# Gate logits of two chunks on VectorE instead of TensorE, and a new order in the later part

## The chip, the cores and the metric

The kernel runs on one core of one Trainium2 chip. The metric is the device time of the whole program in microseconds, as the median of several executions. The core has a matrix engine (TensorE, PE in the profile), a vector engine (VectorE, DVE), a scalar engine (ScalarE, ACT), GpSimd (POOL) and SyncE (SP). Each takes its instructions in order from a queue of its own. Here SP issues nearly all of the transfers, and PEld is the loading of TensorE's stationary operand.

## The reference, cut to what matters

```python
def A(x, wqkv, wo):                     # S = 2048 rows, D = 1024, 32 heads of 32
    q, k, v = heads(x @ wqkv)
    # row s looks at rows s, s-2, ..., s-14 (8 of them); rows before 0 are masked
    attn = softmax(einsum("bhsd,bhswd->bhsw", q, gather(k)) * 32 ** -0.5)
    return einsum("bhsw,bhswd->bhsd", attn, gather(v)).reshape(B, S, D) @ wo

def B(x, w_gate, w_up, w_down):         # Df = 3584
    return (gelu(x @ w_gate) * (x @ w_up)) @ w_down

g = sigmoid((x * gate_w).sum(-1, keepdims=True))   # one number for each row
return g * A(x) + (1 - g) * B(x)
```

All arrays are bfloat16. The change is about `(x * gate_w).sum(-1)`, the gate's logit, and about the order of the work around it.

## The kernel before, in words

The 2048 rows are cut into four chunks of 512 rows, and each chunk into four blocks of 128 (`NST`). Chunks are worked on in pairs, called sup 0 (chunks 0 and 1) and sup 1 (chunks 2 and 3). The large products use a scheme with seven products of half-size blocks in place of eight. It needs sums of blocks of weights and of x beforehand (the "forms", made on VectorE) and sums of products behind (on VectorE and ScalarE, out of PSUM's eight banks).

`main` (L1618) is TensorE's order: q, k and v of the first pair (`qkv_pair`, matmuls at L836), then the hidden layer of the first pair (`ffn`, 28 tiles f, matmuls at L1214), then the output projection of chunk 0 (`down`, L1496), q, k and v of chunks 2 and 3, the hidden layer's first tiles for sup 1 and the projection of chunk 1, the rest of the hidden layer of sup 1, the projection of chunk 2, and that of chunk 3, which is the last stage.

For each tile f of the hidden layer, VectorE and ScalarE do a short chain. L1246 copies a bank to seed the next, L1298 copies one to `u`, L1302 adds a bank to it, L1306 and L1290 are the GELUs, L1263 multiplies GELU and up part, L1272 copies `m`, and L1281 adds a bank and `m` into `hT`, which also frees that bank for TensorE's product two groups later. L504 makes the weights' forms in the ring slots (for sup 0 from raw weights that come with L403; GpSimd stores the forms with L513, and sup 1 loads them back).

Attention works on VectorE in the same time: L1015 and L1021 are the products and sums of the scores, L1107 to L1138 the softmax's sums, L1162, L1172, L1176 and L1180 the weighting of v and its sums. Transposes by DMA on SP's queue (L1084, L1153) carry its weights and results from one layout to another. L369 loads x transposed.

The weights go through a ring of 20 slots of 256 KB (`ring_load`, `ring_give`). A slot is given back in a fixed order by the instruction that read it last, and the next load in `loads` (L438) waits on SP's queue until it has one. Each product m of the projection takes nine such loads (seven of w_down or of its forms, two of wo) and 18 matmuls for each of two column groups g. In the last stage, the third product (m = 2) is replaced by seven smaller ones (`inner`, L1385, 256 columns), whose weights come with three loads of their own (L1335, `load_inner`). It is emitted from hooks inside the other products: `head` after the eighth step of m = 3, g = 1, `body` and `join` before m = 4, g = 0, and `end` inside it.

The gate: `gate(c)` (L930) multiplies x transposed with `gate_w` as 16 matmuls of a 32-column operand for two chunks (L938). VectorE (L953) turns the result round, L961 copies the wanted columns to `zq`, `gate_sum` (L966) adds four partial sums by fp32 matmuls for a pair of chunks (L974), and L979 clips them. The exponential of the logit goes with the first softmax of a chunk (`ez`), and L985 to L991 make `omg`, the factor of the output. `gate(2)` and `gate(3)` stand in the projection of chunk 0, ahead of its product m = 5.

The order of all engines is written out by the class `Weave`. Its `run` (L129) holds some streams of operations and picks again and again the operation with the smallest modelled start plus the stream's bias. An operation with a due date loses its bias from `AHEAD` before that date on. So a bias moves a whole stream behind or ahead of others in an engine's queue, and once the program is built, the queues are fixed:

```python
                b = s[0] if op.due is None or t + self.AHEAD < op.due else 0.0
                b = b if op.bias is None else op.bias
                if best is None or t + b < best[0]:
                    best = (t + b, t, s, op)
```

Of the kernel before, what the change touches and what calls it, by code (L numbers as in the profile page):

```python
# [14 lines left out]
P = 128  # L15
# [28 lines left out]
class Weave:  # L44
# [7 lines left out]
    AHEAD = 15.67  # L52
# [76 lines left out]
    def run(self, streams):  # L129
        live = []  # L130
        for bias, g in streams:
            h = next(g, None)
            if h is not None:
                live.append([bias, g, h])
        while live:
            best = None
            for s in live:
# [4 lines left out]
                b = s[0] if op.due is None or t + self.AHEAD < op.due else 0.0  # L142
# [12 lines left out]
def kernel(  # L155
# [71 lines left out]
    DUE = (80.05, 296.5)  # L227
# [180 lines left out]
    def steps_of(c):  # L408
        return (0, 1, 3, 2, 4, 5, 6) if c >= INNER else range(7)

    def load_down(c, first=()):
        for m in range(7):
# [21 lines left out]
    def loads():  # L434
# [15 lines left out]
        for b in range(2, NBLK):  # L450
            yield from load_block(0, b)
            if 4 + 2 * (b - 1) < NPREP:
                yield load_prep(4 + 2 * (b - 1))
        for sup in range(NSUP):
            c0 = 2 * sup
            more = sup + 1 < NSUP
            if more:
# [7 lines left out]
                for b in range(NE // FB, NBLK):  # L465
                    yield from load_block(sup + 1, b)
            else:
# [49 lines left out]
    def x_forms():  # L517
        t = tt(KH * SC)
        for sup in range(NSUP):
# [11 lines left out]
            yield dve(t, lambda b12=b12, b22=b22: V(out=b12, in0=b22, in1=b12, op=ALU.subtract), [("z", cb)], key=("xf", sup, 3), bias=-1.0 if sup else -0.3)  # L531
            yield dve(t, lambda b21=b21: V(out=tf[:, 2], in0=b21, in1=tf[:, 1], op=ALU.subtract), [t2], key=("xf", sup), bias=-1.0 if sup else -0.3)

    gates, logits = {}, {}
# [205 lines left out]
    def qkv_forms():  # L740
        for sup in range(NSUP):
            c = 2 * sup
            t = tt(D)
            for which in QVK if sup else (0, 1, 2):
# [13 lines left out]
                for f in range(4):  # L758
                    for kt in range(0, KH, 2):
# [17 lines left out]
                        if f == 2 and not sup and which == 0:  # L777
# [3 lines left out]
                                 bias=(0.24, -0.6)[which == 0] if which < 2 and not sup else None,  # L781
                                 due=DUE[1] + 17.6 * QVK.index(which) + 3.94 * f if sup else 0.0)
# [147 lines left out]
    def gate(c):  # L930
# [26 lines left out]
        if c % 2 == 0:  # L957
            logits[c // 2] = (small.tile([P, 2, SC // 32], F32, tag="zq", bufs=1, name="zq"),
                              small.tile([P, 2, NST], F32, tag="zc", bufs=1, name="zc"))
        zq, zc = [z[:, c % 2, :] for z in logits[c // 2]]  # L960
        e = dve(0.1, lambda: nc.vector.tensor_copy(out=zq, in_=zt.rearrange("p (b j) -> p b j", j=32)[:, :, 0]), [e],  # L961
                key=("zq", c))
        yield e
        ez = small.tile([P, NST], F32, tag="ez", bufs=2, name="ez")
        omg = small.tile([P, NST], F32, tag="omg", bufs=3, name="omg")
        gates[c] = (ez, omg, zq, zc)  # L966

    def gate_sum(c):
        i, free = bank_take()
        zq, zc = logits[c // 2]  # L970

        def go():
            for q in range(4):
                nc.tensor.matmul(banks[i][32 * q:32 * (q + 1), 0:2 * NST], lhsT=qsum[:],  # L974
                                 rhs=zq[:].rearrange("p c (j q) -> p (c j) q", q=4)[:, :, q], start=True, stop=True,
                                 tile_position=(0, 32 * q), skip_group_check=True)
        o = pe(1, go, [("zq", c), ("zq", c + 1)] + ([free] if free else []))
# [695 lines left out]
```

## Time and profile before

| what | value |
|---|---|
| times of three runs | 716.2, 716.57, 717.89 us (median 716.57) |
| the profiled execution | 718.17 us, of which the span is 716.4 |
| TensorE busy | 707.4 us, 99% of the span, clock 1.0 throughout |
| VectorE busy | 620.9 us, 87%, 908 instructions |
| ScalarE busy | 327.9 us, 46% |
| GpSimd busy | 73.8 us, 10% |
| DMA | 176.84 MB, mean 247 GB/s; SP's queue 69.0% of 16 engines' span |
| gates of chunks 2 and 3 on TensorE | 16 matmuls from 291.85 to 292.83 us |

All times in the profile are microseconds from the start of the span. A group or a timeline row names the line of the kernel, the engine, the operation, what it writes and reads with its shape, and how often; busy times on one engine may overlap by some tens of nanoseconds, since the next instruction starts before the last has left. The chain is followed from the last instruction back to what released each step.

### The profile page before, as it was taken

The numbers are of one execution on the slowest core, as the hardware profiler recorded it, in microseconds if no ns is written. First come the engines' busy times: TensorE is split into PE (matmuls) and PEld (weight loads), VectorE is DVE, ScalarE is ACT, GpSimd is POOL, SyncE is SP. The second block draws the span as 40 slices with busy tenths as digits, with TensorE's granted clock in tenths as the row PEclk, the third lists the DMA queues.
The fourth block names the chain that finished last, engine by engine and source line by source line (L and its number), as shares of the span: only waits on it lengthen the run. The fifth ranks groups of instructions, "written<-read, shape, count | busy, mean of one in ns | idle before, by whom it ended". The sixth has DMA issues, their size and how long they took to land.

```text
span 716.4 us, 9983 instructions
## 1 busy us (share of the span) xinstructions
PE 707.4 (99%) x3317; PEld 348.4 (49%) x3382; DVE 620.9 (87%) x908; ACT 327.9 (46%) x559; POOL 73.8 (10%) x130
## 2 busy tenths in 40 slices
PE   9999999999999999999999999999999999999998
PEld 5566544444444444456664444444444444444464
DVE  4999999899998989899789988799999997868710
ACT  5454685455675522154465323358556655210110
POOL 0040133433112000100000000100000000001000
PEclk9999999999999999999999999999999999999999
DMA  9963789995998699954369799995647756999972
GB/s 269 374 239 100 223 247 332 355 341 209 220 220 252 201 239 339 331 197 146 85 190 301 256 299 356 311 321 171 178 146 188 180 161 162 307 309 370 398 247 101
DMA packets 181971, 176.84 MB, mean 247 GB/s; under 512 B 56224, under 2 KB 138784, under 8 KB 181664
## 3 DMA queue, kind: packets, MB, share of 16 engines
q1 hardware_dynamic: 172304, 145.53, 69.0%
q0 software_dynamic: 9328, 30.42, 11.4%
q8 instruction: 26, 0.43, 0.2%
q10 hardware_dynamic: 288, 0.26, 0.1%
q14 instruction: 25, 0.20, 0.1%
HBM read 132.65 MB, written 31.46 MB: 229 GB/s over the span
## 4 chain that ended last, share of the span: by engine, by line
PE 87%; DMA 5%; issue 3%; DVE 2%; ACT 1%; POOL 0%; SPq 0%; DVEq 0%; POOLq 0%; ACTq 0%
PE ps L1214 40%; PE ps L1496 27%; PE ps L836 18%; DMA lend<-in_A_x_dram 2%; DMA ring<-in_B_w_gate_dram 1%; PE ps L605 1%; DMA ring<-in_B_w_down_dram 1%; DMA hT<-in_A_wqkv_dram 1%; DMA hT<-in_A_wo_dram 1%; DMA fforms<-ring 0%; DVE ring L504 0%; PE ps L1385 0%; DVE xbuf L1172 0%; POOL fforms L513 0%; ACT hT L1256 0%
## 5 line engine op out<-in xcount | busy, mean ns | idle before, releaser
L1214 PEld LDWEIGHTS <-ring 128*128 128x128 bf16 x1568 | 153.2, 98 | 186.7 <-issue 2.8
L1214 PE MATMUL ps<-lend,ring 128*128 128x512 bf16 x878 | 210.9, 379 | 1.4 <-ACT m L1272 0.4
L1214 PE MATMUL ps<-tf,ring 128*128 128x512 bf16 x658 | 162.7, 379 | 1.1 <-DVE hT L1281 0.3
L1496 PE MATMUL ps<-ring,hT 128*128 128x512 bf16 (+1 forms) x710 | 159.9, 375 | 0.6
L1496 PEld LDWEIGHTS <-hT 128*128 128x128 bf16 x722 | 70.5, 98 | 82.2 <-DVE xbuf L1021 0.4
L836 PEld LDWEIGHTS <-ring 128*128 128x128 bf16 x512 | 65.0, 127 | 46.1 <-issue 1.3
L1162 DVE TENSOR_TENSOR xbuf<-xbuf,lend 128x2048 bf16<-128x2048 bf16 x64 | 77.5, 1216 | 11.4 <-DMA xbuf<-xbuf 11.3
L1015 DVE TENSOR_TENSOR xbuf<-qo,lend 128x2048 bf16<-128x2048 bf16 x64 | 77.0, 1217 | 0.0
L1021 DVE TENSOR_TENSOR xbuf<-xbuf 128x2048 bf16<-128x2048 bf16 x56 | 68.1, 1217 | 0.3
L836 PE MATMUL ps<-tf,ring 128*128 128x512 bf16 x251 | 57.8, 379 | 0.7 <-DVE tf L525 0.5
L836 PE MATMUL ps<-lend,ring 128*128 128x512 bf16 x250 | 57.4, 379 | 0.3
L1246 ACT COPY ps<-ps 128x512 f32<-128x512 f32 x56 | 32.1, 573 | 50.4 <-PE ps L1214 50.3
L1537 ACT ACTIVATE ost<-ps,omg 128x512 bf16<-128x512 f32 x15 | 10.3, 687 | 88.4 <-PE ps L1496 88.4
L1306 ACT ACTIVATE gl<-u 128x512 bf16<-128x512 f32 x56 | 35.4, 632 | 32.0 <-DVE u L1302 31.9
L1496 PE MATMUL ps<-ring,qo 128*128 128x512 bf16 (+1 forms) x191 | 48.9, 375 | 0.3
L1529 POOL DMA_DIRECT2D out_dram<-ost x24 | 13.0, 541 | 341.6 <-ACT ost L1537 252.3
L1290 ACT ACTIVATE gl<-ps 128x512 bf16<-128x512 f32 x56 | 33.5, 599 | 31.7 <-PE ps L1214 31.2
L1263 DVE TENSOR_TENSOR hT<-hT,gl 128x1024 bf16<-128x1024 bf16 x56 | 38.2, 682 | 8.2 <-ACT hT L1256 8.1
L513 POOL DMA_DIRECT2D fforms<-ring x56 | 30.6, 546 | 126.6 <-DVE ring L504 121.4
L504 DVE TENSOR_TENSOR ring<-ring 128x1024 bf16<-128x1024 bf16 x56 | 38.1, 681 | 4.5 <-DMA ring<-in_B_w_up_dram 4.4
L1302 DVE TENSOR_TENSOR u<-ps,u 128x512 f32<-128x512 f32 x56 | 38.3, 683 | 2.8 <-PE ps L1214 2.4
L1172 DVE TENSOR_TENSOR xbuf<-xbuf 128x2048 bf16<-128x2048 bf16 x32 | 38.9, 1215 | 0.1
(149 smaller groups left out, 688.3 us busy)
## 6 DMA issues: line engine op xcount, KB each, us to landing
ring<-dforms SPq DMA_DIRECT2D x105, 256.0 KB, 5.1
ring<-in_B_w_down_dram SPq DMA_DIRECT2D x84, 256.0 KB, 5.3
ring<-in_B_w_gate_dram SPq DMA_DIRECT2D x56, 256.0 KB, 4.5
fforms<-ring POOLq DMA_DIRECT2D x56, 256.0 KB, 5.1
ring<-fforms SPq DMA_DIRECT2D x56, 256.0 KB, 4.0
ring<-in_B_w_up_dram SPq DMA_DIRECT2D x42, 256.0 KB, 4.8
ring<-in_A_wqkv_dram SPq DMA_DIRECT2D x32, 256.0 KB, 3.9
ring<-oforms SPq DMA_DIRECT2D x30, 256.0 KB, 5.5
```

What stands on the lines that cost most here:

```text
L504: nc.vector.tensor_tensor(out=g, in0=ring[:, held[("w", 0, b, x_)], :], in1=ring[:, held[("w", 0, b, y_)], :], op=op)
L836: nc.tensor.matmul(banks[bk][:], lhsT=lhsT, rhs=rhs[:, kt, :], start=(start and kt == 0), stop=(kt == KH - 1), skip_group_check=True)
L1015: V(out=w3(box[t]), in0=q_b, in1=k_w, op=ALU.mult)
L1021: V(out=w3(box[0]), in0=w3(box[0]), in1=w3(box[t]), op=ALU.add)
L1162: return dve(tt(n), taking(("p", t), lambda: V(out=w3(box["p", t]), in0=w3(box["ab"]), in1=v_w, op=ALU.mult)), [("qkv", c, 2, t), abo] + ( ...
L1172: V(out=p0.rearrange("p (u n) -> p u n", u=2), in0=lo, in1=hi, op=ALU.add)
L1214: nc.tensor.matmul(banks[bk][:], lhsT=wv[:, k, fl * P:(fl + 1) * P], rhs=rhs[:, k, :], start=(start and k == 0), stop=(k == KH - 1), skip_ ...
L1263: yield dve(tt(2 * SC), lambda hv=hv, gv=gv: nc.vector.tensor_tensor(out=hv, in0=hv, in1=gv, op=ALU.mult), [e, ev[f, "g1"], ev[f, "g2"]], ...
L1290: nc.scalar.activation(out=gl[f][:, r1 * SC:(r1 + 1) * SC], in_=banks[A[f]][:], func=ACT.Gelu_apprx_tanh)
L1302: e = dve(tt(SC, True), lambda f=f: nc.vector.tensor_tensor(out=u2[f][:], in0=banks[Dk[f]][:], in1=u2[f][:], op=ALU.add), [o, ev[f, "u2"]])
L1306: ev[f, "g2"] = act(0.54, lambda f=f: nc.scalar.activation(out=gl[f][:, r2 * SC:(r2 + 1) * SC], in_=u2[f][:], func=ACT.Gelu_apprx_tanh), [ ...
L1496: nc.tensor.matmul(banks[bk][:, o0:o0 + cols[1] - cols[0]], lhsT=l, rhs=wv[:, i, cols[0]:cols[1]], start=(start and k == 0), stop=(q == la ...
```

## The change: what it does

The logits of chunks 2 and 3 are no longer made from x transposed on TensorE. The rows of x as they lie in memory, four blocks of 128 rows, and `gate_w` repeated for each partition, are loaded into five ring slots for each of the two chunks (`load_rows_of`). VectorE multiplies and sums each block in one call, `tensor_tensor_reduce`, which the built queue shows as two instructions, one over 1024 elements and one over a single element that reads the sum out (`gate_rows`), and clips the four sums. `gate(2)`, `gate(3)` and the second pair's `gate_sum` go; the first pair's `gate_sum` is done for each chunk by itself.

In the last stage, the products are taken in the order 0, 1, 3, 4, 2, 5, 6 rather than 0, 1, 3, 2, 4, 5, 6: the inner product's parts come one product later, its loads stand on SP's queue behind those of m = 3, and the output step L1582 for g = 0 follows the inner join (`joined`).

Last, the streams of `Weave` may have a second bias, which holds from the modelled time 205 us (`TURN`) on; `AHEAD`, a due date and some biases change. By the built queues, VectorE's first 300 or so instructions (to about 205 us) stay nearly as they were and the rest are reordered; GpSimd's queue is the same; on SP's, the transposes L369 of chunks 2 and 3 and the transposes L1084 and L1153 stand a few to ten places later.

```diff
-    AHEAD = 15.67
+    TURN = 205.0
+    AHEAD = 14.59
...
-        for bias, g in streams:
+        for bias, g, *late in streams:
             h = next(g, None)
             if h is not None:
-                live.append([bias, g, h])
+                live.append([bias, g, h, late[0] if late else bias])
...
-                b = s[0] if op.due is None or t + self.AHEAD < op.due else 0.0
+                b = (s[0] if t < self.TURN else s[3]) if op.due is None or t + self.AHEAD < op.due else 0.0
...
-    DUE = (80.05, 296.5)
+    DUE = (80.05, 314.14)
...
     def steps_of(c):
-        return (0, 1, 3, 2, 4, 5, 6) if c >= INNER else range(7)
+        return (0, 1, 3, 4, 2, 5, 6) if c >= INNER else range(7)
 
     def load_down(c, first=()):
-        for m in range(7):
+        for m in (0, 1, 3, 2, 4, 5, 6) if c >= INNER else range(7):
...
         for b in range(2, NBLK):
+            if b == 12:
+                yield from load_rows_of(2)
             yield from load_block(0, b)
...
                 for b in range(NE // FB, NBLK):
                     yield from load_block(sup + 1, b)
+                    if b == 6:
+                        yield from load_rows_of(3)
...
-            yield dve(t, lambda b12=b12, b22=b22: V(out=b12, in0=b22, in1=b12, op=ALU.subtract), [("z", cb)], key=("xf", sup, 3), bias=-1.0 if sup else -0.3)
+            yield dve(t, lambda b12=b12, b22=b22: V(out=b12, in0=b22, in1=b12, op=ALU.subtract), [("z", cb)] if sup == 0 else [], key=("xf", sup, 3), bias=-1.0 if sup else -0.3)
...
-                                 bias=(0.24, -0.6)[which == 0] if which < 2 and not sup else None,
-                                 due=DUE[1] + 17.6 * QVK.index(which) + 3.94 * f if sup else 0.0)
+                                 bias=(0.19, -0.6)[which == 0] if which < 2 and not sup else None,
+                                 due=DUE[1] + 23.67 * QVK.index(which) + 4.11 * f if sup else 0.0)
...
+    def load_rows_of(c):
+        yield ring_load(("gw", c), lambda g: nc.sync.dma_start(out=g, in_=AP(gate_w.tensor, gate_w.offset, [[0, P], [1, D]])))
+        for j in range(NST):
+            yield ring_load(("gx", c, j), lambda g, j=j: nc.sync.dma_start(out=g, in_=x[c * SC + j * P:c * SC + (j + 1) * P, :]))
+
+    def gate_rows():
+        for c in range(2, NCH):
+            zc = small.tile([P, NST], F32, tag="zc", bufs=2, name="zc")
+            ez = small.tile([P, NST], F32, tag="ez", bufs=2, name="ez")
+            omg = small.tile([P, NST], F32, tag="omg", bufs=3, name="omg")
+            gates[c] = (ez, omg, None, zc)
+            for j in range(NST):
+                def dot(c=c, j=j, zc=zc):
+                    r = ring[:, held["gx", c, j], :]
+                    nc.vector.tensor_tensor_reduce(out=r, in0=r, in1=ring[:, held["gw", c], :], scale=1.0, scalar=0.0,
+                                                   op0=ALU.mult, op1=ALU.add, accum_out=zc[:, j:j + 1])
+                o = dve(1.25, dot, [("gx", c, j), ("gw", c)] + ([("ez", c - 2)]), lag=0.5)
+                yield o
+                ring_give(("gx", c, j), o)
+            ring_give(("gw", c), o)
+            yield dve(0.1, lambda zc=zc: nc.vector.tensor_scalar(out=zc[:], in0=zc[:], scalar1=ZMAX, scalar2=-ZMAX, op0=ALU.min,
+                                                                op1=ALU.max), [o], key=("zc", c))
...
-            hk3, hk4 = {7: (head,)}, {0: (body, join), 5: (end,)}
+            hk3, hk4 = {7: (head,)}, {0: (body, join, lambda: joined(0)), 5: (end,)}
+
+        def joined(g):
+            j2, om2, box = 2 * g + 1, omg[:, 2 * g + 1:2 * g + 2], []
+            ev[g, "x"] = dve(0.67, lambda: nc.vector.scalar_tensor_tensor(
+                out=ost_tile(box), in0=banks[Bk[g]][:], scalar=om2, in1=m5[g][:], op0=ALU.mult, op1=ALU.add),
+                [ev[g, "m4"], ev[g, "m5"]])
+            yield from evac(ev[g, "x"], j2, 1, box)
...
-            if (m, g) == (5, 0) and c == 0:
-                yield from gate(2)
-                yield from gate(3)
...
-                    o = yield from prod(Bk[g], m, g, False, [ev[g, "seed"]], hooks=hk3 if g else {})
+                    o = yield from prod(Bk[g], m, g, False, [ev[g, "seed"]])
...
+                    ev[g, "m4"] = yield from prod(Bk[g], m, g, False, [ev[g, "u2"]], hooks=hk4 if g else hk3)
+                    if g or c < INNER:
+                        yield from joined(g)
...
         yield from gate_sum(0)
+        yield from gate_sum(1)
...
-        yield from gate_sum(2)
...
-    w.run([(0.0, main()), (0.0, loads()), (0.0, late_x()), (0.0, moves(3)), (0.6, wforms()), (0.0, down_forms()), (0.0, inner_forms()), (0, x_forms()), (1.89, qkv_forms()),
-           (0.12, preps()), (0.03, attention()), (0.23, scores())])
+    w.run([(0.0, main()), (0.0, loads()), (0.0, late_x()), (0.0, gate_rows(), 0.0), (0.0, moves(3)), (0.6, wforms(), 0.04), (0.0, down_forms(), 0.65), (0.0, inner_forms(), -0.06), (0, x_forms(), -0.44), (1.89, qkv_forms(), -0.92),
+           (0.12, preps()), (0.03, attention(), 0.25), (0.23, scores(), 0.58)])
```

## The prediction, made before any run of the changed kernel

> **What bounds the kernel now.** I read the page's busy table first, then the chain by engine, then windows around each place the change touches, then TensorE's and VectorE's timelines there (start, length, line, operation and count, and in brackets the idle time before it and what ended it). Line numbers are those of the kernel before, for the new order too.
>
> ```profile
> PE 707.4 (99%) x3317; PEld 348.4 (49%) x3382; DVE 620.9 (87%) x908; ACT 327.9 (46%) x559; POOL 73.8 (10%) x130
> PE 87%; DMA 5%; issue 3%; DVE 2%; ACT 1%; POOL 0%; SPq 0%; DVEq 0%; POOLq 0%; ACTq 0%
> ```
>
> TensorE is busy 99% of 716.4 us and holds 87% of the chain: a matmul removed is time removed, unless a wait takes its place. Windows (start:end, length, then busy us and counts of PE, PEld, DVE, ACT, POOL, then granted clock, DMA share, GB/s) show how little room VectorE and the DMA have:
>
> ```profile
> 172.00:204.00 32.00, 31.89 (x146) 14.42 (x148) 31.69 (x51) 21.26 (x37) 6.53 (x12) 1.00 0.85 227
> 204.00:228.00 24.00, 23.42 (x106) 10.45 (x107) 21.36 (x29) 13.37 (x24) 4.32 (x8) 1.00 0.90 225
> 228.00:250.00 22.00, 21.89 (x102) 9.99 (x102) 21.97 (x31) 12.50 (x23) 2.16 (x4) 1.00 0.61 199
> 493.00:546.00 53.00, 52.79 (x243) 24.05 (x246) 50.97 (x66) 32.53 (x57) 0.00 (x0) 1.00 0.62 165
> 644.00:682.00 38.00, 37.84 (x176) 17.32 (x178) 29.29 (x41) 4.58 (x7) 2.70 (x5) 1.00 1.05 383
> ```
>
> The new vector work falls at about 205 to 215 us (rows of chunk 2) and about 493 to 503 us (chunk 3). In both VectorE is nearly full. TensorE's own rows at the removed gates and, below them, where it stands near 220 us:
>
> ```profile
> 291.85 1.05 PE L938 MATMUL ps<-lend,gcol 128*32 128x512 bf16 x16
> 292.83 1.47 PE L1496 MATMUL ps<-ring,hT 128*128 128x512 bf16 x6
> ...
> 218.33 1.89 PE L1214 MATMUL ps<-lend,ring 128*128 128x512 bf16 x8
> 220.48 1.89 PE L1214 MATMUL ps<-tf,ring 128*128 128x512 bf16 x8 [0.26 <-DVE hT L1281]
> 222.21 1.89 PE L1214 MATMUL ps<-lend,ring 128*128 128x512 bf16 x8
> 223.93 1.03 PE L1214 MATMUL ps<-tf,ring 128*128 128x512 bf16 x4
> 225.04 1.89 PE L1214 MATMUL ps<-lend,ring 128*128 128x512 bf16 x7
> 227.01 1.89 PE L1214 MATMUL ps<-tf,ring 128*128 128x512 bf16 x8
> ```
>
> In dense stretches one 512-column matmul takes 0.216 us (49 rows of L1496, one record missing, in 10.74 us). So 218.33 + 8 x 0.216 = 220.06 and the next starts at 220.48: 0.42 lost; likewise 0.25 at 224.79 and 0.24 at 226.77, together 0.91 us. VectorE's timeline names the cause: its L504 waited for block 12's weights, and L1263 and L1281 stood behind it.
>
> ```profile
> 213.52 0.68 DVE L1302 TENSOR_TENSOR u<-ps,u 128x512 f32<-128x512 f32 x1
> 216.80 0.69 DVE L504 TENSOR_TENSOR ring<-ring 128x1024 bf16<-128x1024 bf16 x1 [2.60 <-DMA ring<-in_B_w_up_dram]
> 219.75 0.68 DVE L1281 TENSOR_TENSOR hT<-ps,m 128x512 bf16<-128x512 f32 x1
> ```
>
> **The change, part by part.**
>
> *Gate products gone.* The 16 matmuls hold TensorE from 291.85 to 292.83: **-0.98 us**, on the path. The second gate_sum, at 381 us, goes; the one at 57 us becomes two of four matmuls each, every matmul half as wide (8 took 0.18 to 0.25 us): 0, bounds -0.2 to +0.2. Entering another tile shape may give back a bubble under 0.1.
>
> *Vector work.* Gone: two StreamTransposes (708 ns) and two copies (174 ns), 1.8 us with their gaps. New: eight dots and two clips, one clip more at the start. A dot is two instructions in the built queue, a 1024-element pass and a one-element read-out. Its price p is in no row of before. Low end: L504's 1024 bf16 elements start 0.60 apart, and a clip (156 ns) takes about 0.08 of the queue: p = 0.7. High end: two full passes at one element's pace. That pace is 1.04 ns an element, from L1107's 256 f32 elements (416 ns) and L1302's 512 (683): 1.21 us for 1024, starting 1.14 apart; two passes 2.3. I take one pass at that pace plus a read-out, **p = 1.23** (to 1.4 if the read-out waits for the pass to drain), nearest to L1302, which also carries f32 inside. Eight dots, 10 us, less 1.8, make about 8 us more in VectorE's queue, off the path if the queue has room.
>
> [...] The trace has L504 starting 0.60 apart with 0.68 busy, so I keep 1.23.
>
> *Has the queue room?* In the new order, from 204.70 (unchanged): L504, L1263, L1281, L504, L504 (5 x 0.60) to 207.70; dot, L1302, dot, dot, L1263, L1281 ends at 209.58 + 3p; TensorE needs that bank at 214.0 (212.29 + 8 x 0.216). Then dot, L1302, clip, L504, L1015 (1.14), L1263, L1162 (1.14), L1281 ends at 214.34 + 4p, needed at 220.06. So p may be 1.4 at both. At 1.23 the ends are 213.3 and 219.3: no new wait, and the 2.60 us hole is filled with dots while L504 of block 12 goes to about 223, behind the L1281 it delayed. Hence the three waits vanish: **-0.9 us** (bounds: 0, if others replace them; -0.91). Late next is L504 of block 12 itself.
>
> *Transfers of the rows.* Ten loads of 256 KB join SP's queue, five ahead of block 12 in sup 0, five behind block 6 in sup 1; each holds a ring slot until its dot is done. Block 12's last weights were issued at 211.29 and took 7.22 us (the chain's row):
>
> ```profile
> 211.29 7.22 DMA ring<-in_B_w_gate_dram
> ```
>
> They landed at 218.5. The rows find a place on SP's queue where L369's four transposes (195.47 to 201.05) and nothing else stood, but their slots come back only as the dots end, from 208.9 to 213.9, and SP's issues at 207.58 and 211.89 (3.00 and 3.53 us for two loads) show that it waits for slots. I put block 12's last issue 0.7 to 2.6 us later, landing 219.2 to 221.1, against a need at about 223. If all 1.31 MB lay ahead of it at the stretch's 225 GB/s, it would land at 224.3. Cost 0 (bounds 0 and 1.3 us of VectorE with L1263 and L1281 behind it, all of which TensorE may feel).
>
> Near 500 us the order is L1302, L1138, dot, L1263, L1281, dot, dot, L1302, dot, clip, L1263, L1281. From L1302 at 494.93 the two L1281 end at 498.4 and 503.9 (p = 1.23); TensorE needs them at 500.33 and 506.38: slack 2.0 and 2.4. The rows themselves are issued from 490.2 on and need 4 to 5 us, so the first dot may stand up to 1 us: 0, bounds 0 to +1.
>
> The transposes L369, L1084 and L1153 come up to ten places later on SP; chunk 2's x is needed only at 310 us, and behind L1153 waits L1162, which the order has put later too: 0.
>
> *Last stage.* Before 682 us TensorE has no gap (37.84 of 38.00), so moving the inner product later frees nothing. The order costs: T4's nine loads are wanted 6.8 us sooner (the head and body, 681.72 to 688.48, now follow), from about 681.7 on, the ninth 3.5 us later; they landed at 678 to 683.7 with the inner loads (3 MB, 7.9 us a piece) ahead of T2, which now go behind it. The same bytes lie ahead of T4, in another order: slack 1.5 to 3 us, cost 0, bounds -0.1 to +3. The scores' half of attention gets a bias that ends it about 4.5 us later, at 662.7 for a need at 666.18: covered. L1582's two "x" operations move behind the inner join; L1588's copy still follows the second.
>
> *New order and due dates.* Up to 205 us VectorE's queue is the same but for a few places, so the waits there (0.56 at 138.8, 0.22 at 197) stay. After 228 us its instructions are reshuffled; TensorE's rows there are dense before, so order can gain at most the 0.09 us at 552.8 and the small waits of L836 and L1496, under 1 us. The 8 us more of vector work push attention later there, each L1281 having about 2 us of slack: 0 (bounds -0.9 to +3, a stage's slack lost twice).
>
> **Sum.** -0.98 - 0.9 + 0.1 (bubble) = -1.8 us. The profiled execution took 718.17 us (span 716.4 and 1.8 around it): 716.4 after. It lies 1.6 above the median 716.57, so by the median: **714.8 us**.
>
> **Rivals.**
> *A. Gates only:* the waits at 220 us are replaced by ones like them (L504 late behind the rows). For it: DMA share 0.90 there, SP waiting for slots. Time 716.57 - 1.0 = 715.6.
> *B. Dots too dear (the slower side):* past p = 1.41, L1281 near 219 ends late, 0.4 us for each 0.1 on p; past 1.83 the second one near 504, at the same rate. Against the forecast's -1.8 stands 4 x (p - 1.41) + 4 x (p - 1.83): it decides from p = 1.85, passes +0.3% at 2.1, and gives 716.57 - 1.8 + 3.6 + 1.9 = 720.2 at the high end of 2.3. For it: the operation is in no row, and multiplies and adds. Against: L1302's slope.
> *C. Transfers late:* block 12's weights behind the rows, or T4's in the last stage, by 1 to 5 us beyond their slack: 715.8 to 719.8. For it: share 1.05 in 644 to 682, T2's loads landing as little as 0.7 us ahead of use. Against: the same bytes lie ahead of T4 as before.
> *D. More than forecast:* the new order also takes the small waits after 228 us: 713.0 to 714.4.
> *E. The new order leaves one operation late after 228 us,* where VectorE has 21.97 of 22.00 us busy: up to +3, so 715.6 to 717.8, or 719 if it happens in both pairs of chunks. Against: each of its operations there keeps 2 us.
> *F. The gates were hidden anyway:* excluded, 291.85 to 292.83 is on the chain.
>
> **How the numbers follow.** Forecast 0.40 (own range 713.8 to 715.4), A 0.18, B 0.10, C 0.14, D 0.10, E 0.08. About 0.3% (2.15 us; below 714.42 or above 718.72) is what a measurement of this kernel can tell from no change. Faster: half of the forecast (0.21) and D: 0.31. Slower: most of B (0.07), of C (0.10) and half of E (0.05): 0.22. The rest, 0.47, is within. The low end 713.8 cuts off most of D, 719.2 the ends of B and C; together under 2 in 10.
>
> **What would show it.** No L938 at 292 us, the next product there 1 us sooner; a dot's pair of rows with 1.21 us and a short one, at 1.2 to 1.3 apart; no hole on VectorE at 214 and no wait of L1214 for L1281 at 220; TensorE busy about 706.4. Wrong if the dot takes 1.6 or more, if VectorE stands for ring loads near 222 or 500, or if L1496 waits for a ring load near 681.

## The result, and the profile after

Over 22 executions of each kernel on the same chip the changed kernel took 715.0 us against 716.96 us before (medians). The ratio is 0.9974, with a 95% interval of 0.9964 to 0.9984. That is 0.26% faster: inside the 0.3% that the prediction called no change, and 0.2 us from the time it gave. That it came out so close is partly luck: two of the terms were wrong in opposite directions. The profiled execution took 714.28 us. From here on, lines of the changed kernel have its own numbers: L1238 is the L1214 of before, L1305 is L1281, L1326 is L1302, L1287 is L1263, L509 is L504, L1520 is L1496, L1186 is L1162, and L985 is the new dot.

The page after, busy table and chain by engine:

```profile
span 712.5 us, 9977 instructions
PE 704.5 (99%) x3300; PEld 347.7 (49%) x3366; DVE 631.5 (89%) x920; ACT 329.7 (46%) x559; POOL 74.1 (10%) x130
PE 95%; DMA 3%; issue 1%; SPq 0%; ACT 0%; DVE 0%
```

TensorE carries the chain even more (95%, where it was 87%). VectorE is busy 10.6 us longer (631.5 us, where it was 620.9) and the time still went down. VectorE's timeline where chunk 2's rows are worked on:

```profile
205.12 1.22 DVE L985 CUSTOM_DVE_ANT_0 ring<-ring 128x1024 bf16<-128x1024 bf16 x1
206.27 0.08 DVE L985 DVE_READ_ACCUMULATOR2_ANT zc<- 128x1 f32 x1
206.27 0.68 DVE L1326 TENSOR_TENSOR u<-ps,u 128x512 f32<-128x512 f32 x1
...
209.76 0.68 DVE L1305 TENSOR_TENSOR hT<-ps,m 128x512 bf16<-128x512 f32 x1
...
211.95 0.69 DVE L1326 TENSOR_TENSOR u<-ps,u 128x512 f32<-128x512 f32 x1 [0.38 <-PE ps L1238]
...
216.18 0.69 DVE L1305 TENSOR_TENSOR hT<-ps,m 128x512 bf16<-128x512 f32 x1
```

The dot's pass takes 1.22 us, and the read-out and the next instruction both start 1.15 us after its start: p, the price of a dot in VectorE's queue, is 1.15, and the read-out costs the queue nothing. There is no hole behind L1326. L1305 ends at 210.44 and 216.87. TensorE's timeline in the same place, and where the gates were:

```profile
216.87 1.89 PE L1238 MATMUL ps<-lend,ring 128*128 128x512 bf16 x8
218.59 1.89 PE L1238 MATMUL ps<-tf,ring 128*128 128x512 bf16 x8
220.32 1.89 PE L1238 MATMUL ps<-lend,ring 128*128 128x512 bf16 x8
...
289.38 3.18 PE L1520 MATMUL ps<-ring,hT 128*128 128x512 bf16 x14
292.41 1.03 PE L1520 MATMUL ps<-ring,qo 128*128 128x512 bf16 x4
293.27 2.97 PE L1520 MATMUL ps<-ring,hT 128*128 128x512 bf16 x13
```

Eight matmuls are 1.73 us here, so nothing is lost at 218.59 and 220.32. From 58 us to the last stage this execution has no stop of TensorE of 0.03 us or more. The spans differ by 3.9 us, twice what the medians differ by, so about 2 us of that are not the change. Walking both timelines shows which: TensorE was already 0.65 us ahead at 57 us, and stops of 0.11, 0.56, 0.09 and 0.13 us between 132 and 200 us, in a part of the queues that the change leaves nearly alone, are in the profiled execution of before and not in that of after. Such stops come with the execution and not with the kernel: of eleven profiled executions whose queues are nearly the same up to 200 us, three (this one and two of the experiments) have those at 139, 197 and 200 us, 0.6 to 0.8 us together, and eight have none of them.

### The profile page after: what moved, and what is told of

Read it like the earlier page. It is cut to its first block, busy times and chain, and to the rows that moved or that the text cites. A ratio compares the mean times of both kernels' runs of the same rounds, so it can differ in the third digit from the quotient of the medians.

```text
span 712.5 us, 9977 instructions
## 1 busy us (share of the span) xinstructions
PE 704.5 (99%) x3300; PEld 347.7 (49%) x3366; DVE 631.5 (89%) x920; ACT 329.7 (46%) x559; POOL 74.1 (10%) x130
## 4 chain that ended last, share of the span: by engine, by line
PE 95%; DMA 3%; issue 1%; SPq 0%; ACT 0%; DVE 0%
PE ps L1238 47%; PE ps L1520 28%; PE ps L841 18%; DMA ring<-in_A_wqkv_dram 1%; DMA lend<-in_A_x_dram 1%; PE ps L1409 1%; DMA hT<-in_A_x_dram 1%; DMA ring<-dforms 0%; PE ps L610 0%; SPq L439 0%; DVE tf L530 0%; PE ps L943 0%; ACT ost L1634 0%; ACT it L1425 0%; PE ps L1000 0%
## 5 line engine op out<-in xcount | busy, mean ns | idle before, releaser
L1238 PEld LDWEIGHTS <-ring 128*128 128x128 bf16 x1568 | 153.4, 98 | 184.9
L1238 PE MATMUL ps<-lend,ring 128*128 128x512 bf16 x878 | 210.9, 379 | 0.9
L1238 PE MATMUL ps<-tf,ring 128*128 128x512 bf16 x659 | 162.9, 379 | 0.7
L1520 PE MATMUL ps<-ring,hT 128*128 128x512 bf16 (+1 forms) x706 | 160.0, 375 | 0.8
L1520 PEld LDWEIGHTS <-hT 128*128 128x128 bf16 x722 | 70.6, 98 | 82.0
L1186 DVE TENSOR_TENSOR xbuf<-xbuf,lend 128x2048 bf16<-128x2048 bf16 x64 | 77.7, 1217 | 2.7 <-DMA xbuf<-xbuf 2.5
L1520 PE MATMUL ps<-ring,qo 128*128 128x512 bf16 (+1 forms) x192 | 49.1, 375 | 0.2
L1287 DVE TENSOR_TENSOR hT<-hT,gl 128x1024 bf16<-128x1024 bf16 x56 | 38.2, 683 | 5.6 <-ACT hT L1280 5.4
L1326 DVE TENSOR_TENSOR u<-ps,u 128x512 f32<-128x512 f32 x56 | 38.4, 686 | 3.5 <-PE ps L1238 2.5
L1305 DVE TENSOR_TENSOR hT<-ps,m 128x512 bf16<-128x512 f32 x56 | 38.3, 684 | 2.4 <-PE ps L1238 2.2
L1322 ACT COPY u<-ps 128x512 f32<-128x512 f32 x56 | 32.8, 586 | 15.5 <-PE ps L1238 15.5
L1196 DVE TENSOR_TENSOR xbuf<-xbuf 128x2048 bf16<-128x2048 bf16 x32 | 38.9, 1216 | 0.1
```

Of the source, the lines that this page charges most:

```text
L1186: return dve(tt(n), taking(("p", t), lambda: V(out=w3(box["p", t]), in0=w3(box["ab"]), in1=v_w, op=ALU.mult)), [("qkv", c, 2, t), abo] + ( ...
L1196: V(out=p0.rearrange("p (u n) -> p u n", u=2), in0=lo, in1=hi, op=ALU.add)
L1238: nc.tensor.matmul(banks[bk][:], lhsT=wv[:, k, fl * P:(fl + 1) * P], rhs=rhs[:, k, :], start=(start and k == 0), stop=(k == KH - 1), skip_ ...
L1287: yield dve(tt(2 * SC), lambda hv=hv, gv=gv: nc.vector.tensor_tensor(out=hv, in0=hv, in1=gv, op=ALU.mult), [e, ev[f, "g1"], ev[f, "g2"]], ...
L1305: ev[f, "up2"] = dve(tt(SC, True), lambda f=f: nc.vector.tensor_tensor(out=hs(f, 1), in0=v3(banks[Bk[f]][:]), in1=v3(m5[f][:]), op=ALU.add ...
L1322: nc.scalar.copy(out=u2[f][:], in_=banks[Bk[f]][:])
```

## Experiments

The theory taken into them is the prediction's: each part does its own share, that is, the gates' products and the waits at 220 us go with the gate part, and the order and the last stage's move are worth nothing. The rivals: the waits go because of the order; they were in the one profiled execution only; or the last stage's move pays.

**The gate part alone**

```diff
# before, with gate(2), gate(3) and gate_sum(2) out; load_rows_of, gate_rows and gate_sum(1) in
-    w.run([(0.0, main()), (0.0, loads()), (0.0, late_x()), (0.0, moves(3)), ...
+    w.run([(0.0, main()), (0.0, loads()), (0.0, late_x()), (0.0, gate_rows()), (0.0, moves(3)), ...
```

> The kernel before with the gate part alone: logits of chunks 2 and 3 from rows on VectorE, gate_sum for each chunk by itself, the old biases and the old last stage. Parts theory (each part does its own share): TensorE loses 1.07 us of products and bubbles at 292 us and 0.27 us at 381 us, and pays 0.06 at 57 us; and the dots fill VectorE's hole at 214 us, so the 0.9 us of waits at 219 to 227 us are gone: 2.2 us under the kernel before, and TensorE's timeline dense from 219 to 228 us. Order theory (the waits go because of the new biases): only 1.3 us under before, with waits of L1214's products near 220 us left. Chance theory (the waits at 220 us came up in the one profiled execution only): 1.3 us under before, with no wait near 220 us.

Measured: 715.59 us against 717.11, ratio 0.9984 (0.9974 to 0.9994): 1.15 us under by the ratio and 1.5 by the medians, not 2.2. No wait is left near 220 us, but there are four new ones, 0.24 us at 242 (for L504's form), 0.12 and 0.17 at 556 and 562, and 0.29 in the last stage near 675 us. The chain in the last stage of this kernel:

```profile
670.72 5.29 DMA ring<-oforms
...
676.05 1.24 PE ps L1519 x5
```

The load of wo's forms for m = 3 landed late. SP had stood from 657.89 to 661.22 with the inner product's load (L1335 of before) at its head, whose buffer attention used until 661.20; in the kernel before attention was done with it at 656.99. By the clock the forms are not later than in the kernel before (issued at 670.05 after 671.19), but TensorE comes to the head of the inner product 2.2 us sooner, and SP gained only half of that. So the gate part takes TensorE's products away and pays for some of it in waits that the kernel before has not.

**The last stage's move alone**

```diff
-        return (0, 1, 3, 2, 4, 5, 6) if c >= INNER else range(7)
+        return (0, 1, 3, 4, 2, 5, 6) if c >= INNER else range(7)
...
-        for m in range(7):
+        for m in (0, 1, 3, 2, 4, 5, 6) if c >= INNER else range(7):
# and the hooks of head, body, join and end, and joined(g), as in the change
```

> The kernel before with the last stage's third product behind its fifth, and nothing else. Parts theory: 0, within 0.3 us, since TensorE's rows are dense before 690 us in both kernels; the loads for the fifth product land in time. Rival (the move is what pays): 0.5 us or more under before. Rival (the order of the loads costs, and the other parts hide it): 0.5 us or more over, with waits of L1496's products for ring loads near 682 us. Up to 640 us this is the queue of before, so its profile is also a second look at the waits at 132 to 200 us and at 219 to 227 us: the parts theory expects the latter 0.9 us again, the chance theory not.

Measured: 716.67 us against 717.11, ratio 0.9993 (0.9982 to 1.0004): no difference that these runs can tell. Its profile is worth more than its time, since up to 640 us it is the queue of before, seen once more. Its timelines of VectorE and TensorE:

```profile
214.81 0.69 DVE L504 TENSOR_TENSOR ring<-ring 128x1024 bf16<-128x1024 bf16 x1 [1.88 <-DMA ring<-in_B_w_up_dram]
...
217.75 0.68 DVE L1281 TENSOR_TENSOR hT<-ps,m 128x512 bf16<-128x512 f32 x1
```

```profile
217.14 1.89 PE L1214 MATMUL ps<-lend,ring 128*128 128x512 bf16 x8
218.87 1.89 PE L1214 MATMUL ps<-tf,ring 128*128 128x512 bf16 x8
...
289.86 1.05 PE L938 MATMUL ps<-lend,gcol 128*32 128x512 bf16 x16
290.84 2.33 PE L1496 MATMUL ps<-ring,hT 128*128 128x512 bf16 x10
```

VectorE has the same hole, 1.88 us in place of 2.60, but the stop of TensorE behind it is gone. Of the 0.91 us that the prediction removed near 220 us, only 0.11 us (at 224.7) is there, and of the 0.89 us between 132 and 200 us nothing. The chance theory is right for most of it.

**The changed kernel with the old last stage**

```diff
-        return (0, 1, 3, 4, 2, 5, 6) if c >= INNER else range(7)
+        return (0, 1, 3, 2, 4, 5, 6) if c >= INNER else range(7)
# load_down's order, the hooks and the output step back as before
```

> The changed kernel with the old last stage. Parts theory: as the changed kernel, 2.0 us under before, within 0.3 us. If the last stage's move pays only together with the new order (attention ends later there), this is 0.5 us or more over the changed kernel, with a wait near 666 or 682 us.

Measured: 716.04 us against 717.11, ratio 0.9983 (0.9972 to 0.9994), where the changed kernel has 0.9974; the two intervals overlap, so the profile has to say whether it is real. SP's timeline, VectorE's end of attention, and the chain:

```profile
658.06 1.12 SPq L431 DMA_DIRECT2D ring<-in_A_wo_dram  x2
662.42 1.52 SPq L1359 DMA_DIRECT2D xbuf<-dforms  x2
```

```profile
661.18 1.22 DVE L1196 TENSOR_TENSOR xbuf<-xbuf 128x2048 bf16<-128x2048 bf16 x1
```

```profile
672.13 5.36 DMA ring<-oforms
...
677.54 1.24 PE ps L1520 x5
```

SP was done with the loads ahead at 659.18 and stood until 662.42: the inner product's load (L1359) needs a buffer of attention's, and attention's L1196 ended at 662.40. Behind it on the same queue stand the nine loads for m = 3, which then come late: three stops of 0.19, 0.25 and 0.25 us at 676 to 677.5 us. That this is real rests on the row at 662.42 and on the same hold in the run of the gate part alone, more than on the time. The profiled execution took 717.38 us, 1.3 above its median, and TensorE stops for 1.6 us more ahead of 640 us, 0.97 of it here:

```profile
456.19 2.36 DVE L1186 TENSOR_TENSOR xbuf<-xbuf,lend 128x2048 bf16<-128x2048 bf16 x2 [4.40 <-DMA xbuf<-xbuf]
```

```profile
467.07 1.89 PE L1238 MATMUL ps<-lend,ring 128*128 128x512 bf16 x8 [0.81 <-ACT m L1296]
```

Up to there the queues of all engines are those of the changed kernel, whose profile has none of it (there VectorE waited 1.32 us for that transfer, and TensorE not at all): it is this execution. In the kernel before, the same load was issued at 660.06, 0.3 us behind the one ahead of it. The changed kernel has the m = 3 loads in front:

```profile
662.84 1.00 SPq L431 DMA_DIRECT2D ring<-oforms  x2
664.19 1.00 SPq L1359 DMA_DIRECT2D xbuf<-dforms  x2
```

**The inner loads behind m = 3, the products left where they were**

```diff
# on top of the run before
             if m == 2 and c >= INNER:
-                yield from load_inner()
                 continue
...
+            if m == 3 and c >= INNER:
+                yield from load_inner()
```

> The changed kernel with the old last stage, except that the inner product's three loads stand on SP's queue behind the nine loads of m = 3, as in the changed kernel. Queue theory (with attention later, the inner loads wait for their buffer at the head of SP's queue and hold up the loads of m = 3 behind them; moving the loads is what the last stage's move is worth): no wait of L1496's products near 676 us, and the time of the changed kernel, about 0.7 us under the run with the old last stage. Rival (the product itself has to come later, because its forms are then late): the wait goes from 676 us to the head at about 681 us, and the time is that of the run with the old last stage or more.

Measured: 714.83 us against 716.88, ratio 0.9974 (0.9963 to 0.9985), as the changed kernel. No stop from 58 us to the last stage. The profile bears the queue theory out: what the last stage's move is worth is three loads put behind nine others, and no gain is seen from the product coming later. By the times alone the two runs can't be told apart (0.9983 and 0.9974, overlapping intervals).

**The changed kernel without its order part**

```diff
-    TURN = 205.0
-    AHEAD = 14.59
+    AHEAD = 15.67
...
# DUE, the due dates, 0.19 and all second biases back as before
```

> The gate part and the last stage's move with the old biases, AHEAD and due dates: the changed kernel without its order part. By the run of the gate part alone, which had waits of 0.24 us at 241 us (for a form, L504), 0.12 and 0.17 at 556 and 562 us and 0.29 at 675 us, the last of these should go and the others stay: 0.4 to 0.6 us over the changed kernel, 1.4 to 1.6 under before. If the order part is worth nothing here: as the changed kernel. If it is worth more than these waits show: 1 us or more over it.

Measured: 715.31 us against 716.88, ratio 0.9978 (0.9970 to 0.9987), 0.3 us over the changed kernel by the ratio and by the medians, a little less than expected and within the noise. Its profile has no stop near 675 us, the 0.24 us at 241 us again, and 0.47, 0.10, 0.13 and 0.09 at 465 to 556 us. Up to the last stage VectorE's, ScalarE's and SP's queues are those of the gate part alone, so the two profiles show one order twice: the 0.24 at 241 and 0.09 to 0.12 near 556 us are in both, 0.3 us together. The others are in one of them only, and the stop near 465 us, again for ScalarE's copy `m`, stood in the changed kernel with the old last stage too, whose order is the new one.

**The order part alone**

```diff
# before, with TURN, AHEAD = 14.59, the due dates and
-    ... (0.6, wforms()), (0.0, down_forms()), ... (0.03, attention()), (0.23, scores())])
+    ... (0.6, wforms(), 0.04), (0.0, down_forms(), 0.65), ... (0.03, attention(), 0.25), (0.23, scores(), 0.58)])
```

> The kernel before with the second biases, TURN, AHEAD and the due dates alone. Its queue still has two L504 ahead of the L1281 that was late at 220 us. Parts theory: the waits near 220 us stay in some form, 0.3 to 0.9 us of them, and the time is that of before within 0.5 us. Order theory: the waits are gone, 0.9 us under before. A third way: the biases were set for a queue with the dots in it, and without them something else is late: up to 2 us over before, with a wait on TensorE that the kernel before has not.

Measured: 749.38 us against 717.11, ratio 1.0449 (1.0429 to 1.0469). The third way, and more than ten times its size. What TensorE waited for, in that kernel's waits by line (total, times, longest; L1455 is the forms of the projection, L1454 of before):

```profile
PE ps L1497 <- DVE qo L1455: 14.4, 3, 6.6
PE ps L1497 <- DVE hT L1455: 7.8, 1, 7.8
```

**The same with the late bias of the projection's forms at 0**

```diff
-    ... (0.0, down_forms(), 0.65), ...
+    ... (0.0, down_forms()), ...
```

> The order part alone, as in the run that took 749 us, but without the late bias of 0.65 for the projection's forms (down_forms, L1454 of the kernel before), which goes back to 0 throughout. Starving theory: that run's waits of the projection's products for these forms (1.9 us at 298, 7.9 at 429, 6.7 at 461 and 6.2 at 654 us) come because attention, at a late bias of 0.25, is taken first as long as some of it is ready; without the 0.65 they go, and the time is 716 to 721 us. Rival (attention itself is late by the other biases, and the forms wait for it): the waits stay in the main, 735 us or more.

Measured: 741.73 us against 717.19, ratio 1.0333 (1.0298 to 1.0367). Both theories hold half. None of the four waits for the forms is left, so these were starved by the late bias; but attention now ends late instead, and the last stage waits for it (L1181 writes attention's result):

```profile
PE ps L1497 <- DVE qo L1181: 13.0, 2, 9.7
PE ps L1497 <- DMA ring<-dforms: 5.2, 1, 5.2
```

The biases give a good order only to the set of operations they were written beside. Why attention falls behind without the dots was not followed further.

**A dearer dot, twice**

```diff
+                    for _ in range(1):      # range(2) in the second run
+                        V(out=r, in0=r, in1=r, op=ALU.min)
                     nc.vector.tensor_tensor_reduce(out=r, in0=r, ...
```

> The changed kernel with one more VectorE instruction ahead of each dot, the minimum of a row block with itself (1024 bf16 elements, 0.60 us of the queue each by L504's pace), which leaves the data as it is: a dot then takes 1.15 + 0.60 = 1.75 us of the queue. The prediction's sum put the threshold at 1.41 and so expects 4 x 0.34 = 1.4 us near 219 us. The trace after has the dots' chain 1.1 us earlier than that sum, and slack 1.72 at L1281 behind the fourth dot, with 0.5 us of idle time ahead of it: 4 x 0.60 - 0.5 - 1.72 = 0.2 us near 219 us, nothing near 502 us (slack 2.6 against 2.4). Cheap theory (VectorE has room, the dots' price does not matter): 0. If instead the pushed-back attention is what costs: 1 us or more, in places behind 250 us.

> The same with two such instructions ahead of each dot, 2.35 us for each. By the prediction's sum 3.8 us near 219 us and 2.1 near 502 us, 5.9 in all. By the trace after: 4 x 1.20 - 0.5 - 1.72 = 2.6 us near 219 us and 4.8 - 2.6 = 2.2 near 502 us, 4.8 in all, as waits of L1214's products for L1281. Cheap theory: 0 to 0.5. If pushed-back attention costs as well: 6 us or more, with waits behind 250 us or in the last stage.

Measured: one more instruction 717.5 us against 716.88, ratio 1.0013 (0.9998 to 1.0028); two more 725.06, ratio 1.0114 (1.0097 to 1.0131). VectorE's and TensorE's timelines of the first, then TensorE's of the second:

```profile
205.81 0.68 DVE L986 TENSOR_TENSOR ring<-ring 128x1024 bf16<-128x1024 bf16 x1
206.53 1.23 DVE L987 CUSTOM_DVE_ANT_0 ring<-ring 128x1024 bf16<-128x1024 bf16 x1
```

```profile
217.67 1.89 PE L1240 MATMUL ps<-lend,ring 128*128 128x512 bf16 x8
219.97 1.89 PE L1240 MATMUL ps<-tf,ring 128*128 128x512 bf16 x8 [0.41 <-DVE hT L1307]
```

```profile
218.01 2.62 PE L1240 MATMUL ps<-tf,ring 128*128 128x512 bf16 x8 [2.89 <-DVE hT L1307]
220.42 2.89 PE L1240 MATMUL ps<-lend,ring 128*128 128x512 bf16 x8
223.15 1.03 PE L1240 MATMUL ps<-tf,ring 128*128 128x512 bf16 x4
```

The added instruction costs 0.72 us of the queue and not 0.60: the dot, which needs its result, starts 0.72 us behind it (206.53 - 205.81), where instructions that do not need each other's results start 0.60 apart (in the same profile L1328 at 207.68 and the next L986 at 208.28). So p = 1.87 and 2.59. At p = 1.87 the wait near 219 us sits where the sums put it, at L1281's bank (L1307 here): 0.57 us, for 4 x 0.72 - 0.5 - 1.72 = 0.7 by the slack of the trace after. The 0.39 us near 502 us are at another place than the sums had:

```profile
502.68 1.89 PE L1240 MATMUL ps<-lend,ring 128*128 128x512 bf16 x8 [0.23 <-ACT m L1298]
```

TensorE waits there for ScalarE's copy `m` (L1272 of before), which follows the GELU of the `u` that VectorE's L1302 finishes, and three dots stand ahead of that L1302. In the trace after the copy ends at 499.11 and TensorE wants it at 500.91, so 3 x 0.72 - 1.80 = 0.36 us. That L1281's bank would have given 4 x 0.72 - 2.6 = 0.3 is a coincidence. A further 0.58 us at 516 us is the first L1188 behind the fourth dot, which waits for a late transpose with L1307 behind it. At p = 2.59 the stops near 212 to 222 us are 3.6 us, 3.0 of it at L1307, against 5.76 - 0.5 - 1.72 = 3.5. From 508 to 525 us they are again 3.6: 2.57 for the copy `m`, against 3 x 1.44 - 1.80 = 2.5, and 0.64 and 0.41 at two L1307 behind it. The other 2.2 us of that execution's stops lie before 205 us, where the queue is that of the changed kernel. The median is 10 us over the changed kernel, where 4.8 to 5.9 were expected; the slowed clock of the last section is 1.7 of that. That VectorE has room to spare is refuted: from p = 1.7 or so on (1.75 near 502 us), TensorE pays.

**Carried on: chunk 1's logit from rows as well, with chunk 2's rows in three other places**

```diff
-            yield from gate(1)
-        yield from gate_sum(1)
...
-        for c in range(2, NCH):
+        for c in range(1, NCH):
...
             if b == 12:
-                yield from load_rows_of(2)
+                yield from load_rows_of(1)
# load_rows_of(2) behind the second (first run) or third matrix (second run), or ahead of the first (third run)
```

> The changed kernel carried on: chunk 1's logit from rows too. Its exponential runs only at 284 us, so its rows take the place of chunk 2's (ahead of block 12, dots near 205 us), and chunk 2's rows, whose exponential runs at 431 us, are loaded between the second and third weight matrix of q, k, v for sup 1 (dots near 340 us, where VectorE is busy 14.4 of 20 us). TensorE loses the second gate product, 0.67 us at 16 us, and half of gate_sum at 57 us, about 0.25: 0.9 us under the changed kernel. Rivals: early waits on VectorE take it back (the product at 16 us covers the forms of x): 0 to 0.3 under; or the new loads and dots are late near 340 us, where TensorE runs on q, k and v: 1 us or more over.

> The same with chunk 2's rows behind the third weight matrix (dots near 360 us, where VectorE is busy 17.6 of 20 us): 0.9 us under the changed kernel, or, if the place of the dots matters, up to 1 us worse than the run before it.

> The same with chunk 2's rows ahead of the first weight matrix of q, k, v (dots near 300 us, where VectorE is busy 17.4 of 20 us and the DMA share is 1.03 before that): 0.9 us under the changed kernel if the loads are in time; 0.5 us or more over the other two if the weights behind the rows are late for L776's forms near 310 us.

Measured: 725.49, 725.93 and 729.49 us against 717.01, ratios 1.011 (1.0092 to 1.0128), 1.0122 (1.0102 to 1.0143) and 1.0162 (1.0138 to 1.0186). All three miss by 8 us and more, and the largest stop of all three is at the same place, near 219 us (4.6, 3.7 and 3.8 us; the third has one of 3.8 at 416 us as well). SP, VectorE and TensorE in the first:

```profile
188.26 5.58 SPq L370 DMA_TRANSPOSE lend<-in_A_x_dram  x4
204.21 1.26 SPq L1178 DMA_TRANSPOSE xbuf<-xbuf  x1
...
208.77 2.94 SPq L975 DMA_DIRECT2D ring<-in_A_x_dram  x4
```

```profile
214.63 0.68 DVE L511 TENSOR_TENSOR ring<-ring 128x1024 bf16<-128x1024 bf16 x1
216.34 1.23 DVE L986 CUSTOM_DVE_ANT_0 ring<-ring 128x1024 bf16<-128x1024 bf16 x1 [1.03 <-DMA ring<-in_A_x_dram]
...
222.12 0.69 DVE L511 TENSOR_TENSOR ring<-ring 128x1024 bf16<-128x1024 bf16 x1
```

```profile
217.45 1.03 PE L1239 MATMUL ps<-tf,ring 128*128 128x512 bf16 x4
222.87 2.74 PE L1239 MATMUL ps<-lend,ring 128*128 128x512 bf16 x6 [4.40 <-DVE ring L511]
```

An attention transpose stood at the head of SP's queue from 193.84 until 204.21, so the rows were issued at 208.77; in the changed kernel the first of them was issued at 194.61. The dots waited for them, and the form L511 (the L504 of before) that TensorE needed stood behind four dots: 4.40 us. Taking gate(1) out had rearranged the early order too, with stops of 1.0 us near 168 us. The main line of the expectation took both places to be as in the changed kernel, which was wrong: the order is made anew for every set of operations.

## Why the prediction was right, and where not

*Gates.* Forecast -0.98 and +0.1 for a bubble. By the last L1496 product ahead and the first behind, the gates occupied 290.84 - 289.55 - 0.216 = 1.07 us in the run of the last stage alone. The bubbles of about 0.09 us are where the tile shape changes from 128*128 to 128*32 (289.77 to 289.86 there, 380.90 to 380.99 us in the profile before), so they go with the gates: that term had the wrong sign.

*gate_sum.* Forecast 0. At 381 us it occupied 381.17 - 380.68 - 0.216 = 0.27 us, with the bubbles, and that is gone. At 57 us the split costs 0.06 us. So -0.2, at the end of the bounds; together TensorE's work is 1.3 us shorter, where the sum had 0.9.

*The waits at 220 us.* Forecast -0.9. The mechanism was seen rightly (L504 ahead of L1281, a hole that the dots fill), but the term was mis-sized: 0.91 us in the profiled execution, 0.11 in the other one of the same queue. The failed step is to take a single execution's waits for the kernel's, and then to subtract them from a median that lies 1.6 us under that execution. The two errors, 0.4 us too little for the products and up to 0.8 too much for the waits, go in opposite ways. That the forecast lies 0.2 us from the median is to that extent luck.

*The dot and the queue.* Forecast p = 1.23 (bounds 0.7 and 2.3) and a threshold of 1.41. Measured 1.15, and the threshold near 1.7 by the trace after. The step that was off is "from 204.70 (unchanged)": in the execution before, VectorE's queue was itself 1.1 us behind TensorE there. In the trace after, L1305 (the L1281 of 205.91) ends 6.0 us ahead of the group of four matmuls at 209.96; before, 4.8 ahead of that at 211.43. Near 219 us the law of rival B, 4 us for each us of p beyond the threshold, held in both runs with dearer dots. Near 502 us the prediction had the wrong operation: the wait is for the copy `m` behind three dots and L1302, 3 us for each us of p beyond 1.75, ahead of L1281's bank, to which it gave 4 beyond 1.83. Rival B was right as a mechanism and its price was not reached. The eight passes have a median of 1.214 us, where the prediction's slope of 1.04 ns an element, from two rows of before, had 1.21. Its p = 1.4, for a read-out that waits for the pass to drain, was the author's estimate, and no trace here shows such a wait: in that after, the read-out and the next instruction both start 0.07 us before the pass ends (206.27 against 206.34).

*Rows' transfers.* Forecast 0, and 0 was measured. Rival C did not happen in this kernel. In the one of its three relatives that is shown it was the rows themselves that came late, 14 us (208.77 for 194.61), and not block 12's weights behind them.

*Last stage.* Forecast 0 for the move, and alone it is 0. In company it is not: the gate part pushes attention back. The prediction costed a later end of attention by one of its readers, TensorE at 666.18, and called it covered (it is: attention ends near 661 us). It did not ask who else waits for attention: the inner loads' buffer, and behind these on SP's queue the loads for m = 3. Rival C had named these (T2's, landing as little as 0.7 us ahead of use), but for their share of the DMA and not for this hold. The wait of 0.3 to 0.7 us, in both profiles with the rows and the old order of the loads and in none with the new one, is what the move takes away.

*New order.* Forecast 0, with bounds of -0.9 to +3. With the rows the run without it is 0.3 us slower, which is within the noise but is also the sum of the two waits (241 and 556 us) that both profiles of the old order have and none of the new; by itself it costs 32 us. The bounds, put on the change as a whole, held; "the order" has no price of its own.

So the gate part is worth 1.3 us of TensorE's time, of which it keeps about as much when it comes alone (1.15 to 1.5 us under, with 0.4 to 1.9 by the interval), and the other two parts mostly prevent what it would bring on. The median gained 2.0 us (1.1 to 2.6 by the interval), while the undisturbed profiles of the last stage alone (span 714.4) and of the inner loads moved (712.8) differ by 1.6. Where the rest comes from is not settled, since a few profiles do not tell how often the waits near 132 to 227 us come up in each kernel.

## What to carry to other kernels

A wait in a single profile of a kernel that is 99% busy is to be seen a second time before it is put into a sum, above all when that execution is slower than the median. When an operation moves later, list everything that waits for its buffers, transfers at the head of a shared queue included, and not only the bottleneck engine. Where a greedy planner writes the order, a set of biases has no worth apart from the operations it was made for, so parts of such a change can't be priced one by one, nor can the change be carried on without setting them again.

## What the runs showed of the hardware

A wait of TensorE can cost more than its length, and need not: of the five waits below, of 2.33 to 4.40 us, three were followed by a lower granted clock and two were not. In the run with two more instructions for each dot, the granted clock after the 2.89 us wait, and in the first run with chunk 1's rows after the 4.40 us wait (windows: length, busy and count of PE, PEld, DVE, ACT and POOL, granted clock, DMA share, GB/s):

```profile
218.00:221.00 3.00, 2.99 (x10) 1.24 (x10) 2.93 (x5) 0.00 (x0) 0.00 (x0) 0.67 0.02 5
221.00:224.00 3.00, 3.00 (x12) 1.14 (x11) 3.00 (x6) 2.19 (x4) 0.54 (x1) 0.76 0.72 203
224.00:228.00 4.00, 4.00 (x20) 1.86 (x19) 4.00 (x5) 2.09 (x4) 0.00 (x0) 1.00 0.55 176
```

```profile
223.00:226.00 3.00, 3.00 (x8) 1.06 (x7) 2.15 (x3) 0.00 (x0) 0.54 (x1) 0.50 1.19 291
226.00:229.00 3.00, 3.00 (x10) 1.09 (x8) 2.00 (x3) 1.70 (x3) 0.00 (x0) 0.57 1.18 301
229.00:232.00 3.00, 3.00 (x16) 1.35 (x15) 2.33 (x5) 1.22 (x3) 0.23 (x1) 1.00 0.93 243
```

In the first, the 16 matmuls from 218.01 to 223.15 took 5.14 us where 3.46 (16 x 0.216) is usual: 1.7 us more. But in these runs the length of the wait does not decide it alone. In the same run the wait of 2.41 us at 508 us left the clock at 1.00 (the execution's mean clock, 0.998 over 723.3 us, is 1.4 us in all by the rounded figure, no more than the stretch above), and in the third run with chunk 1's rows one of 3.65 us, to 420.40, left it at 1.00 while one of 2.33 us, to 479.67, did not:

```profile
420.40:424.40 4.00, 3.95 (x18) 1.86 (x20) 4.00 (x5) 1.29 (x3) 0.00 (x0) 1.00 0.12 45
479.60:483.60 4.00, 3.93 (x11) 1.50 (x11) 4.00 (x6) 1.38 (x4) 0.00 (x0) 0.57 1.12 374
```

Two shorter waits left the clock at 1.00 as well: 0.45 us, to 15.29, in the kernel before (14 to 18 us), and 0.41 us, to 219.97, in the run with one more instruction for each dot (219 to 222 us). What decides it is not shown here. The lower clock is one reason why the prediction's rates for rival B, which count the waits alone, fall short for the largest p, and part of why the runs with long waits lost more than their waits.
